# Second pass of a two-layer product by a seven-product block scheme on 768-token chunks

## The chip, the cores and the metric

One core of a Trainium2 chip. The metric is the device time of one execution, in microseconds (us); lower is better. Engines: PE (TensorE, matrix products), DVE (VectorE), ACT (ScalarE), POOL (GpSimd) and SP (SyncE, which here issues every DMA).

## What is computed

```python
scores = scale * np.matmul(q, k.transpose(0, 1, 3, 2))      # 8 batches, 8 heads, 576 tokens, head size 64
scores = np.where(mask, scores + bias[None], -1e9)           # causal window of 128, a linear bias per head
attn = softmax(scores); attn_out = np.matmul(attn, v)
x = attn_out.transpose(0, 2, 1, 3).reshape(4608, 512)
h = x @ w_in                                                 # 512 x 2048
sp = np.maximum(h, 0.0) + np.log1p(np.exp(-np.abs(h)))
out = (h * erf(sp)) @ w_out                                  # 2048 x 512
```

The weights arrive as 64-bit floats. Every operand of the two products is split into a high and a low float32r part, and a product is three: high by high, high by low, low by high.

## The kernel before

Attention is 48 steps, one for each of 12 chunks of 384 tokens and 4 pairs of heads: scores on PE (L614; the first eight steps have other forms), bias and minimum on DVE (L648), exponentials on ACT (L656), the inverse of the sums on DVE (L670, L671), the normalisation on POOL (L679), a transpose on DVE (L696), the product with v on PE (L718). Its output x goes to DRAM and, for the first chunks, stays in SBUF.

The 2048 columns of the first product are 16 ff tiles of 128, too many for SBUF beside attention, so they are done in two passes. **Pass one** runs beside attention and after it: 12 chunks x `NF1` = 7 tiles = 84 units of 384 tokens. A unit has its first products (`unit`, 12 matrix products, L926), a copy from PSUM (L908 on ACT or L912 on DVE), for a round of five units softplus and erf on ACT with their table loads (L963, L965), the product with h, the split into `gh` and `gl` on DVE (L975, L912, L979), and the second products (`products`, 9 for a unit, L997) that add to one PSUM bank for each 128 tokens. The partial outputs go to DRAM (`pd`). **Pass two** does the other 9 tiles on 9 chunks of 512 tokens, 81 units of 12 first and 12 second products of 512 columns, reads the partial outputs back, adds them (L1019) and stores (L1024).

`Weights.prepare` turns a 128 x 512 tile of weights into its two halves: two operations on ACT (L802, or POOL; L809), shift, sign and addition on DVE (L812, L814, L816), the high half (L908, L912 or POOL) and the low half on DVE (L823). Pass one's fourteen tiles come at the start; pass two's eighteen come when attention has closed its pools (`gone`), and stay in SBUF.

The order on every engine is fixed when the program is built. Code makes operations with costs, reads, writes and a due time `at`; `Plan.run` gives each free engine the operation that is ready and due first. Every engine then runs its own list in order and waits by semaphores; SP's list holds all DMA issues. A tile of a pool waits until the one that had its place is read. PSUM has eight banks: `o0` to `o2` for sums, `h` for first products in pass one, four `s` for attention and then for pass two.

Of the kernel before, what the change touches and what calls it, by code (L numbers as in the profile page):

```python
# [19 lines left out]
P = 128  # L20
# [22 lines left out]
PB, XB, OB, TB = 3, 3, 3, 2  # L43
QB, VB = 4, 2
# [12 lines left out]
W2A, W2B = 60, 2.0  # L57
# [94 lines left out]
SUB = ALU.subtract  # L152
# [228 lines left out]
def dve(n, fast=False):  # L381
    return 0.1 + n * (0.00054 if fast else 0.00108)
# [391 lines left out]
class Weights:  # L774
# [10 lines left out]
    def prepare(self, which, f, at, after=()):  # L785
# [4 lines left out]
        r = Buf(self.stage, [P, DM], I32, "wt", 2, f"wu{nm}")  # L790
        t = Buf(self.stage, [P, DM], I32, "wt", 2, f"wt{nm}")
# [5 lines left out]
        flt = lambda x: x.all.bitcast(F32)  # L797
        V = nc.vector

        def lower(e):  # L800
            if e == "Act":
                nc.scalar.mul(flt(q), words(1).bitcast(F32), 2.0**-112)  # L802
            else:
                nc.gpsimd.tensor_scalar(flt(q), words(1).bitcast(F32), 2.0**-112, 1.0, op0=ALU.mult, op1=ALU.mult)
# [3 lines left out]
        def units(e):  # L808
# [8 lines left out]
        pool, tag = self.place(which, f)  # L817
        hi = Buf(pool, [P, DM], F32R, "h" + tag, 1, "wh" + nm)
        lo = Buf(pool, [P, DM], F32R, "l" + tag, 1, "wl" + nm)
        op({**({} if f < POOLH else {"Act": act(DM), "DVE": dve(DM, True)}), "Pool": pool_cast(DM)},  # L820
           lambda e: Moe.copy(self, e, hi.all, flt(t)),
            r=[t, *after], w=[hi], at=at)
        op({"DVE": dve(DM)}, lambda e: V.tensor_tensor(lo.all, flt(t), hi.all, SUB),  # L823
            r=[t, hi, *after], w=[lo], at=at)
        self.t[which, f] = (hi, lo)


class Moe:
# [4 lines left out]
    def __init__(self, tc, plan, ctx, x_dram, part_dram, out):  # L833
# [11 lines left out]
        for nf, size, width, tail in zip((NF1, NF - NF1), UPR, (CH, CH2), ((), TAIL)):  # L845
            n = nf * (self.nt // width) - sum(tail)
            self.rounds += [size] * (n // size) + [n % size] * (n % size > 0) + [*tail]

    def one_pass(self, weights, first, width, accs, time, x_pool=None, after=()):

        self.first, self.width = first, width
        self.x_pool, self.after = x_pool or self.xp, list(after)
# [19 lines left out]
    def load_x(self, c, at):  # L872
        nc, op, W = self.nc, self.plan.op, self.width
        if self.first and c in self.raw:
            raw = self.raw[c]
            parts = [p for cc, p in self.direct_parts if cc == c]
            halves = [[p for p in parts if p.at[1] // 2 == k2] for k2 in range(2)]
        else:
            raw = Buf(self.x_pool, [P, NK, W], F32, "xr", 1, f"xr{c}_{int(self.first)}")
            pieces, pos = [], c * W  # L880
            while pos < (c + 1) * W:
                d, off = divmod(pos, CH)
                n = min(CH - off, (c + 1) * W - pos)
                pieces.append((d, off, pos - c * W, n))
                pos += n

            def load(e):
                for d, off, to, n in pieces:
                    nc.sync.dma_start(raw[:, :, to : to + n], self.x_dram[d][:, :, off : off + n])

            op(emit=load, r=[*self.after, *(x for d, *_ in pieces for x in self.x_parts[d])], w=[raw],
               at=at - XL, **dma(P * NK * W * 4, len(pieces)))
            halves = [[raw], [raw]]
        x = []
        for k2 in range(2):
# [3 lines left out]
            op({"DVE": dve(2 * W, True), "Act": act(2 * W), **({} if self.first and c >= POOLX else {"Pool": pool_cast(2 * W)})},  # L899
# [48 lines left out]
    def flush(self):  # L948

        nc, op, W = self.nc, self.plan.op, self.width  # L950
        units, self.round = self.round, []
        V, A, G = nc.vector, nc.scalar, nc.gpsimd
        total = len(units) * W
        pairs = []
        for i, hs in enumerate(self.hs):
            u = units[i * MW // W]
            s = Buf(self.hp, [P, MW], F32, "m", MB, f"s{u['U']}", keep=KS)
            pairs.append((min(MW, total - i * MW), hs, s, u["at"] + MC, u["U"]))
        first = self.first

        def tables(e):
            for n, hs, s, at, U in pairs:
                A.activation(s[:, :n], hs[:, :n], AF.Softplus)  # L963
            for n, hs, s, at, U in pairs:
                A.activation(s[:, :n], s[:, :n], AF.Erf)  # L965
# [4 lines left out]
           r=[p[1] for p in pairs], w=[p[2] for p in pairs], at=pairs[0][3])  # L970
        g = []
        for n, hs, s, at, U in pairs:
            gh = Buf(self.hp, [P, MW], F32R, "m", MB, f"gh{U}", keep=1)
            gl = Buf(self.hp, [P, MW], F32R, "m", MB, f"gl{U}", keep=0)
            op({"DVE": dve(n)}, lambda e, s=s, hs=hs, n=n: V.tensor_tensor(hs[:, :n], s[:, :n], hs[:, :n], ALU.mult),  # L975
                r=[s, hs], w=[hs], at=at)
            op({"DVE": dve(n, True), "Act": act(n), **({} if first and pairs[0][4] >= POOLG else {"Pool": pool_cast(n)})},
# [4 lines left out]
        for j, u in enumerate(units):  # L982
            self.products(u, j * W, g)
# [176 lines left out]
```

## Time and profile before

| | |
|---|---|
| median of three runs | 984.11 us (981.88 to 984.54) |
| profiled execution | span 983.3 us from the first to the last instruction; the page gives no other time of it |
| PE | 955.2 us busy, 97% |
| DVE, ACT, POOL | 561.1, 608.3, 149.3 us busy |
| DMA | 115.09 MB, mean 117 GB/s |

Busy time is that in which an engine has an instruction under way. A matrix product's record runs on into the next one's, so the price of one is the distance between starts. Attention ends at about 400 us, the last first product of pass one is at 520 us.

### The profile page before, as it was taken

Reading aid. Unit: us, or ns where it says so; the run is one execution under the profiler, and the core shown is the slowest. Engines: PE = TensorE matmul, PEld = TensorE weight load, DVE = VectorE, ACT = ScalarE, POOL = GpSimd, SP = SyncE. Lnnn points to the kernel's source line nnn. Section 1 sums busy time; section 2 is a strip of 40 time slices with the busy share of each in tenths; the row PEclk is TensorE's granted clock in tenths of the full one; section 3 lists DMA queues with packets and bytes.
Section 4 is the critical chain, followed back from the end, with each engine's and each line's share of the span. In section 5 each row is a group of like instructions: output and inputs, shape, how many; then the busy total and the mean of one; then the engine's idle time right before and its main releaser. Section 6 shows DMA issues by size and latency. Waiting matters only on the chain.

```text
span 983.3 us, 25856 instructions
## 1 busy us (share of the span) xinstructions
PE 955.2 (97%) x10936; PEld 801.7 (82%) x10936; DVE 561.1 (57%) x1336; ACT 608.3 (62%) x1245; POOL 149.3 (15%) x297
## 2 busy tenths in 40 slices
PE   8788999999999999999999999999999999999997
PEld 6577877888888888989998888888888888888886
DVE  6877885776667666774389434343434343434342
ACT  7878885678667865786688563636363636363552
POOL 3444333333233323000001000000000000000000
PEclk9988999999999999999999999999999999999999
DMA  6675555547555552551034112121212121212021
GB/s 232 217 220 178 171 188 169 184 144 226 180 165 171 184 192 87 199 168 37 33 116 142 64 43 86 43 86 43 87 43 86 43 86 43 86 43 86 1 65 43
DMA packets 52932, 115.09 MB, mean 117 GB/s; under 512 B 5584, under 2 KB 22736, under 8 KB 52816
## 3 DMA queue, kind: packets, MB, share of 16 engines
q1 hardware_dynamic: 52816, 113.43, 36.1%
q8 instruction: 86, 1.41, 0.6%
q14 instruction: 30, 0.25, 0.1%
HBM read 85.10 MB, written 28.31 MB: 115 GB/s over the span
## 4 chain that ended last, share of the span: by engine, by line
PE 81%; ACT 6%; DVE 4%; POOL 3%; DMA 3%; issue 2%; SPq 0%; ACTq 0%; POOLq 0%; DVEq 0%
PE banks L997 37%; PE banks L926 36%; PE banks L718 5%; POOL p L679 3%; PE banks L614 3%; DMA wri<-w_in 2%; ACT p L656 1%; DVE pa L696 1%; ACT s L963 1%; DMA tables<-bias 1%; ACT s L965 1%; ACT L965 1%; ACT L963 1%; ACT L967 0%; ACT wui L809 0%
## 5 line engine op out<-in xcount | busy, mean ns | idle before, releaser
L926 PE MATMUL banks<-xh,whi 128*128 128x384 f32 (+1 forms) x660 | 245.6, 372 | 8.2 <-ACT hs L908 5.5
L926 PE MATMUL banks<-xh,wli 128*128 128x384 f32 (+1 forms) x660 | 240.9, 365 | 1.3 <-DVE wli L823 1.3
L926 PE MATMUL banks<-xl,whi 128*128 128x384 f32 (+1 forms) x660 | 240.7, 365 | 0.0
L997 PE MATMUL banks<-who,gh 128*128 128x512 f32 x576 | 229.6, 399 | 0.5 <-DVE ot L912 0.5
L997 PE MATMUL banks<-wlo,gh 128*128 128x512 f32 x576 | 225.3, 391 | 0.3 <-issue 0.3
L997 PE MATMUL banks<-who,gl 128*128 128x512 f32 x576 | 225.4, 391 | 0.0
L908 ACT COPY hs<-banks 128x384 f32<-128x384 f32 (+2 forms) x127 | 58.4, 468 | 224.0 <-PE banks L926 223.9
L679 POOL TENSOR_SCALAR p<-p,st 128x160 f32<-128x160 f32 (+2 forms) x282 | 139.0, 514 | 228.1 <-DVE st L671 175.4
L926 PEld LDWEIGHTS banks<-xh,whi 128*128 128x128 f32 x660 | 125.1, 190 | 31.1 <-ACT hs L908 7.7
L912 DVE COPY hs<-banks 128x512 f32<-128x512 f32 (+2 forms) x66 | 37.8, 573 | 190.1 <-PE banks L926 170.2
L926 PEld LDWEIGHTS banks<-xl,whi 128*128 128x128 f32 x660 | 125.4, 190 | 15.5
L926 PEld LDWEIGHTS banks<-xh,wli 128*128 128x128 f32 x660 | 125.1, 190 | 14.1 <-DVE wli L823 1.7
L656 ACT ACTIVATE p<-p,st 128x160 f32<-128x160 f32 (+2 forms) x288 | 120.5, 423 | 25.1 <-DVE st L648 23.5
L997 PEld LDWEIGHTS banks<-who,gh 128*128 128x128 f32 x576 | 108.1, 188 | 27.7 <-issue 6.3
L997 PEld LDWEIGHTS banks<-who,gl 128*128 128x128 f32 x576 | 108.1, 188 | 23.5 <-DVE hs L975 0.5
L997 PEld LDWEIGHTS banks<-wlo,gh 128*128 128x128 f32 x576 | 108.1, 188 | 19.3
L975 DVE TENSOR_TENSOR hs<-s,hs 128x768 f32<-128x768 f32 (+1 forms) x106 | 89.9, 884 | 17.3 <-ACT s L965 17.3
L648 DVE CUSTOM_DVE_ANT_0 p<-banks,tables 128x160 f32<-128x160 f32 (+2 forms) x288 | 75.3, 319 | 31.3 <-PE banks L614 30.8
L979 DVE TENSOR_TENSOR gl<-hs,gh 128x768 fp32r<-128x768 f32 (+1 forms) x106 | 91.0, 888 | 0.7
L963 ACT ACTIVATE s<-hs 128x768 f32<-128x768 f32 (+1 forms) x106 | 76.5, 776 | 0.5
L965 ACT ACTIVATE s<-s 128x768 f32<-128x768 f32 (+1 forms) x106 | 76.4, 776 | 0.5
L718 PEld LDWEIGHTS banks<-pa,v 32*64 32x64 f32 x4576 | 59.5, 132 | 14.5 <-issue 8.6
(66 smaller groups left out, 874.5 us busy)
## 6 DMA issues: line engine op xcount, KB each, us to landing
v<-v_b SPq DMA_DIRECT2D x24, 512.0 KB, 4.0
xr<-xd SPq DMA_DIRECT2D x14, 768.0 KB, 4.9
qk<-qk SPq DMA_DIRECT2D x24, 400.0 KB, 4.1
pd<-ot SPq DMA_DIRECT2D x36, 256.0 KB, 3.8
ot<-pd SPq DMA_DIRECT2D x36, 256.0 KB, 3.4
wri<-w_in SPq DMA_DIRECT2D x16, 512.0 KB, 4.2
qk<-qk SPq DMA_DIRECT2D x16, 512.0 KB, 4.6
wro<-w_out SPq DMA_DIRECT2D x16, 512.0 KB, 4.1
```

Of the source, the lines that this page charges most:

```text
L648: nc.vector.tensor_tensor_reduce(out=dst(j), in0=cut(ps[j].all), in1=cut(table[:, half * j + c0 : half * j + c0 + n]), scale=-0.125, scala ...
L656: nc.scalar.activation(dst(j), dst(j), AF.Exp, bias=low[:, j : j + 1], scale=-1.0, accum_out=total[:, j : j + 1])
L679: (nc.vector if e == "DVE" else nc.gpsimd).tensor_scalar(dst, dst, totals[t][:, j : j + 1], 1.0, op0=ALU.mult, op1=ALU.mult)
L718: nc.tensor.matmul(whole[64 * j : 64 * j + 64, first + a, 32 * t0 : 32 * (t0 + n)], lhsT=y.v[rows, 128 * slot + 64 * j : 128 * slot + 64 * ...
L908: self.nc.scalar.copy(out, src)
L912: self.nc.vector.tensor_copy(out, src)
L926: nc.tensor.matmul(ps[:, :W], lhsT=ww[:, cs], rhs=xx[:, k], start=(k2 + k + n == 0), stop=(k2 + k + n == 4),)
L963: A.activation(s[:, :n], hs[:, :n], AF.Softplus)
L965: A.activation(s[:, :n], s[:, :n], AF.Erf)
L975: op({"DVE": dve(n)}, lambda e, s=s, hs=hs, n=n: V.tensor_tensor(hs[:, :n], s[:, :n], hs[:, :n], ALU.mult), r=[s, hs], w=[hs], at=at)
L979: op({"DVE": dve(n)}, lambda e, gh=gh, gl=gl, hs=hs, n=n: V.tensor_tensor(gl[:, :n], hs[:, :n], gh[:, :n], SUB), r=[hs, gh], w=[gl], at=at)
L997: nc.tensor.matmul(po.all, lhsT=gg[:, cs], rhs=w.all, start=(u["start"] and n == 0), stop=(u["end"] and n == 2),)
```

## The change

`NF1` is 6, so pass one has 72 units. Pass two works on 6 chunks of 768 tokens and 5 pairs of ff tiles, 30 rounds. For a round the first product of a pair (256 columns of w_in) with 768 tokens is cut into blocks in all three dimensions: 128 columns, 256 of the 512 inner rows, 384 tokens. Eight block products become seven, on sums and differences of blocks. The sums of w_in are made once for a pair, beside attention (`Weights.pair`: four sums, then `split`), and written split to DRAM with the split w_out; each round reads 1.84 MB of `wi` and 1.05 MB of `wo` (`fetch`, with three places for each). The differences of x are made once for a chunk (`load_blocks`). The seven products go into two banks `z`; products that share a sum add to a bank whose content has been copied out between them. Six banks hold the sums of the second product. Parts of x and every third `wi` lie where pass one's weights were.

```diff
-NF1 = 7
-UPR = (5, 3)
+NF1 = 6
+UPR = 5
+NP = (NF - NF1) // 2
+LEFT = {"A11": (0, 512), "A12": (256, 768), "S1": (1024, 1536), "S2": (1280, 1792),
+        "S3": (2048, 2560), "S4": (2304, 2816), "A22": (3072, 3328)}
...
+    def split(self, name, src, n, r, to, at):
+        nc, op = self.nc, self.plan.op
+        wb = Buf(self.stage, [P, 2, DM], F32R, "wb", WB, name)
+        op({"Act": act(n), "DVE": dve(n, True), "Pool": pool_cast(n)},
+           lambda e: Moe.copy(self, e, wb[:, 0, :n], src()), r=r, w=[wb], at=at)
+        op({"DVE": dve(n)}, lambda e: nc.vector.tensor_tensor(wb[:, 1, :n], src(), wb[:, 0, :n], SUB),
+           r=[*r, wb], w=[wb], at=at)
+        op(emit=lambda e: nc.sync.dma_start(
+            to.ap.rearrange("p (two n) -> p two n", two=2), wb[:, :, :n].bitcast(F32)),
+           r=[wb], w=[to], at=at, **dma(2 * P * n * 4))
+
+    def pair(self, p, f, wi, wo, at):
+        t1, t2 = (self.decode(0, f + j, at) for j in range(2))
...
+            eng.tensor_tensor(s1, a21, a22, ADD)
+            eng.tensor_tensor(s2, s1, a11, SUB)
+            eng.tensor_tensor(s3, a11, a21, SUB)
+            eng.tensor_tensor(s4, a12, s2, SUB)
+
+        op({"DVE": 4 * dve(SB), "Pool": 4 * pool_tt(SB)}, add, r=[t1, t2], w=[sums], at=at)
...
+    def blocks_pass(self, wi, wo, pool, home, gone, time):
+        tags = ["o0", "o1", "o2", "h", "a0", "a1"]
+        R = 0
+        for C in range(self.nt // (2 * CH)):
+            x = self.load_blocks(C, time(R), pool, home, gone)
+            po = [Buf(self.ps, [P, DM], F32, tag, 1, f"q{C}_{tag}") for tag in tags]
+            for p in range(NP):
+                own, over = home["wi"] if R % 3 == 2 else (Buf(pool, [P, 14 * SB], F32, "wi", 2, f"wi{R}"), [])
+                a = self.fetch(wi[p], own, over * (R == 2), 14 * SB, gone, time(R) - WL)
+                own = Buf(pool, [P, 4 * DM], F32, "wo", 3, f"wo{R}")
+                b = self.fetch(wo[p], own, [], 4 * DM, gone, time(R) - WL + 0.6 * TR)
+                self.pair(C, p, R, x, a, b, po, time(R))
+                R += 1
...
+        z, v, u = (Buf(self.ps, [P, 512], F32, "z", 2, f"{k}{R}") for k in "zvu")
+        product(z, "A11", "B11", True)
+        read(z, h[0][0])
+        product(v, "A12", "B21", True)
+        add(v, h[0][0])
+        product(z, "S2", "T2", False)
+        read(z, h[0][1])
+        product(u, "S1", "T1", True)
+        product(z, "S3", "T3", False)
+        read(z, h[1][1])
+        add(u, h[1][1])
+        product(u, "S4", "B22", False)
+        add(u, h[0][1])
+        product(z, "A22", "T4", False)
+        read(z, h[1][0])
+        g = self.activate([(MW, hs[j], h[j], at + MC, f"{R}_{j}") for j in range(2)])
...
+                    for n, (gg, k) in enumerate(((gh, 0), (gh, 1), (gl, 0))):
+                        nc.tensor.matmul(
+                            po[t].all, lhsT=gg[:, cs], rhs=w[k],
+                            start=(first and j + n == 0), stop=(last and j + n == 3),
...
-        home = self.op_ if self.first or t % 2 else self.x_pool
-        ot = Buf(home, [P, DM], F32, "o", OB, f"ot{T}_{u['U']}")
+        ot = Buf(self.op_, [P, DM], F32, "o", OB, f"ot{T}_{u['U']}")
...
+    for p in range(NP):
+        w1.later = [attention.loaded[min(WN + p * WD, len(attention.loaded) - 1)]]
+        w1.pair(p, NF1 + 2 * p, wi[p], wo[p], W2A + p * W2B)
```

`product` is six matrix products of 384 columns. A round's PE work stands in the order like this. Before, PE in pass two: a unit's first products on the halves of x (`xh`, `xl`), then another unit's second products.

```order
L926 MATMUL banks<-xh_1_10085,whi_7254 128x512
L926 MATMUL banks<-xl_1_10087,whi_7254 128x512
L926 MATMUL banks<-xh_1_10085,wli_7261 128x512
L997 MATMUL banks<-who_8248,gh_10046 128x512
L997 MATMUL banks<-wlo_8259,gh_10046 128x512
L997 MATMUL banks<-who_8248,gl_10056 128x512
```

Now, PE in a round of pass two (L1158 are block products, `yh`, `yl` and `w_551` the parts of x, `wi` the weights; L1196 second products in groups of three):

```order
L1158 MATMUL banks<-yl_2_10286,wi_10301 128x384
L1158 MATMUL banks<-yh_2_10243,wi_10301 128x384
L1158 MATMUL banks<-w_551,wi_10301 128x384 x6
L1196 MATMUL banks<-wo_10333,gh_0_10479 128x512 x2
L1196 MATMUL banks<-wo_10333,gl_0_10486 128x512
L1158 MATMUL banks<-w_551,wi_10301 128x384 x6
L1196 MATMUL banks<-wo_10333,gh_0_10479 128x512 x2
L1196 MATMUL banks<-wo_10333,gl_0_10486 128x512
L1196 MATMUL banks<-wo_10333,gh_1_10484 128x512 x2
L1196 MATMUL banks<-wo_10333,gl_1_10494 128x512
L1158 MATMUL banks<-w_551,wi_10301 128x384 x12
```

The second products of a round stand among the first products of the round two later, one or two groups between block products, the other eight behind them.

DVE in an attention step, before, from the inverse of one step to the transpose of the next (the rows of L648 between them are left out where they repeat):

```order
L696 STREAM_TRANSPOSE pa_5744<-p_5591 128x960
L648 ISA p_5730,st_5731<-banks,tables_320_857 128x160
L648 ISA st_5731 128x1
```
```order
L670 TENSOR_SCALAR st_5731<-st_5731 128x6
L671 RECIPROCAL st_5731<-st_5731 128x6
L518 COPY xs_5845<-banks 128x384
L696 STREAM_TRANSPOSE pa_5877<-p_5730 128x960
```

Now, DVE at such a place (L859 makes low halves of pass two's weights, L1032 and L1036 are the old L975 and L979, L717 the transpose):

```order
L717 STREAM_TRANSPOSE pa_4624<-p_4442 128x960
L691 TENSOR_SCALAR st_4580<-st_4580 128x6
L692 RECIPROCAL st_4580<-st_4580 128x6
L1036 TENSOR_TENSOR gl_4643<-hs_1_4092,gh_4567 128x768
L1032 TENSOR_TENSOR hs_2_4354<-s_4360,hs_2_4354 128x384
L859 TENSOR_TENSOR wb_4427<-ws_4385,wb_4427 128x512
L859 TENSOR_TENSOR wc_4588<-ws_4385,wc_4588 128x512
L717 STREAM_TRANSPOSE pa_4723<-p_4579 128x960
```

Between an inverse and the transpose behind it, while POOL normalises, there now stand operations of the units and of pass two's weights.

SP at the end, before (`ot` with `pd` is the load of a partial output, `out_dram` a store):

```order
L1018 DMA ot_164_10979<-pd_114 128x512
L1018 DMA ot_164_10984<-pd_115 128x512
L1024 DMA out_dram<-ot_164_10654 32x512 x2
L1024 DMA out_dram<-ot_164_10654 64x512
L1024 DMA out_dram<-ot_164_10659 128x512
L1024 DMA out_dram<-ot_164_10979 64x512 x2
L1024 DMA out_dram<-ot_164_10984 128x512
```

And now:

```order
L1079 DMA out_dram<-ot_29_11255 32x512
L1079 DMA out_dram<-ot_29_11263 64x512
L1079 DMA out_dram<-ot_29_11263 32x512 x2
L1079 DMA out_dram<-ot_29_11271 32x512 x2
L1079 DMA out_dram<-ot_29_11271 64x512
L1073 DMA ot_29_11576<-pd_113 128x512
L1073 DMA ot_29_11578<-pd_114 128x512
L1073 DMA ot_29_11580<-pd_115 128x512
L1079 DMA out_dram<-ot_29_11576 128x512
L1079 DMA out_dram<-ot_29_11578 64x512 x2
L1079 DMA out_dram<-ot_29_11580 128x512
```

The last three loads of partial outputs stood ahead of the last stores; now they stand behind the stores of the first half of the chunk, whose buffers they take.

## Rows read from the trace of the kernel before

**Rows 1.** Busy time by stage: stretch, length, busy us (instructions) of each engine, granted clock, DMA.
```profile
core 0: us, PE busy (x) PEld busy (x) DVE busy (x) ACT busy (x) POOL busy (x), PEclk, DMA share, GB/s
0.00:100.00 100.00, 82.62 (x1602) 68.63 (x1603) 75.82 (x276) 76.22 (x232) 41.00 (x80) 0.90 0.66 213
...
405.00:517.00 112.00, 111.65 (x559) 100.70 (x558) 69.86 (x106) 82.70 (x122) 2.31 (x2) 1.00 0.32 111
517.00:958.00 441.00, 441.00 (x1949) 365.58 (x1949) 202.35 (x269) 227.75 (x286) 3.29 (x3) 1.00 0.21 66
```
**Rows 2.** Waits of PE from 400 us: who for whom, us, times, longest.
```profile
PE banks L926 <- ACT hs L908: 0.3, 1, 0.3
```
**Rows 3.** Timeline of PE, the first products of two units in pass one.
```profile
403.03 0.34 PE L926 MATMUL banks<-xh,whi 128*128 128x384 f32 x1
...
407.22 0.33 PE L926 MATMUL banks<-xh,whi 128*128 128x384 f32 x1
```
**Rows 4.** Chain that ended last, its end: start us, us, what.
```profile
956.21 2.72 PE banks L926 x12
958.93 19.05 PE banks L997 x84
...
978.00 0.69 DVE ot L1019
```
**Rows 5.** Timeline of PE, scores of the 17th and the last attention step.
```profile
129.18 1.05 PE L614 MATMUL banks<-qk 64*32 64x160 f32 x48
...
388.15 1.05 PE L614 MATMUL banks<-qk 64*32 64x160 f32 x48
```
**Rows 6.** Busy time by stretch in the attention stage.
```profile
88.00:100.00 12.00, 12.00 (x210) 10.61 (x209) 9.85 (x28) 8.41 (x24) 6.69 (x11) 1.00 0.69 217
100.00:120.00 20.00, 19.25 (x394) 15.75 (x392) 16.83 (x47) 18.76 (x45) 5.99 (x10) 1.00 0.45 143
120.00:130.00 10.00, 7.86 (x204) 6.26 (x188) 9.01 (x24) 8.00 (x21) 4.50 (x6) 1.00 0.70 239
130.00:150.00 20.00, 19.89 (x329) 16.49 (x313) 16.64 (x47) 14.90 (x37) 7.43 (x13) 1.00 0.58 181
...
129.18:388.15 258.97, 256.81 (x5876) 214.45 (x5875) 173.16 (x586) 177.08 (x512) 90.68 (x192) 1.00 0.55 172
```
**Rows 7.** Waits of DVE from 129 to 388 us.
```profile
DVE p L648 <- PE banks L614: 27.7, 15, 4.5
DVE pa L696 <- POOL p L679: 20.7, 21, 1.6
```
**Rows 8.** Groups of instructions by line and shape: copies from PSUM.
```profile
L908 ACT COPY hs<-banks 128x384 f32<-128x384 f32 x60 | 28.4, 474 | 37.3 <-PE banks L926 37.3
L912 DVE COPY hs<-banks 128x384 f32<-128x384 f32 x24 | 13.3, 554 | 29.5 <-PE banks L926 29.3
```
**Rows 9.** Timeline of SP near the end: issues of eleven stores.
```profile
944.04 5.79 SPq L1024 DMA_DIRECT2D out_dram<-ot  x11
```
**Rows 10.** DMA issues: how many, KB each, median us to landing.
```profile
ot<-pd SPq DMA_DIRECT2D x36, 256.0 KB, 3.4
...
out_dram<-ot SPq DMA_DIRECT2D x14, 256.0 KB, 2.1
```
**Rows 11.** Groups of DVE: decoding of weights and low halves.
```profile
L823 DVE TENSOR_TENSOR wlo<-wto,who 128x512 fp32r<-128x512 f32 x16 | 11.3, 709 | 0.3
L814 DVE SCALAR_TENSOR_TENSOR wti<-wqi,wti 128x512 int32<-128x512 int32 x16 | 11.2, 701 | 0.4
L816 DVE CUSTOM_DVE_ANT_0 wti<-wti,wui 128x1024 uint16<-128x1024 uint16 x16 | 11.2, 698 | 4.1 <-ACT wui L809 3.4
L812 DVE TENSOR_SCALAR wti<-wqi 128x512 int32<-128x512 int32 x16 | 7.0, 437 | 0.6
L979 DVE TENSOR_TENSOR gl<-hs,gh 128x256 fp32r<-128x256 f32 x3 | 1.3, 421 | 0.0
```
**Rows 12.** Groups of POOL, from 100 to 150 us and from 200 to 388 us.
```profile
L679 POOL TENSOR_SCALAR p<-p,st 128x160 f32<-128x160 f32 x25 | 15.8, 650 | 22.6 <-DVE st L671 14.5 <-ACT wuo L809 8.1
...
L679 POOL TENSOR_SCALAR p<-p,st 128x160 f32<-128x160 f32 x141 | 65.1, 483 | 123.2 <-DVE st L671 97.1 <-ACT gh L908 17.4 <-ACT ot L908 8.8
```

More of the change, by code (lines that the diff above doesn't have):

```diff
@@ L783, in __init__, with decode @@
         self.t = {}
-    def prepare(self, which, f, at, after=()):
+    def decode(self, which, f, at):
         nc, op = self.nc, self.plan.op
@@ L844, in __init__, with one_pass @@
         self.rounds = []
[L845 to L852, printed above, removed]
+        n = NF1 * (self.nt // CH)
+        self.rounds += [UPR] * (n // UPR) + [n % UPR] * (n % UPR > 0)
+    def one_pass(self, weights, accs, time):
+        self.first, width = True, CH
+        self.width, self.after = width, []
         fs = weights.ffs
@@ L873, in load_x @@
         nc, op, W = self.nc, self.plan.op, self.width
-        if self.first and c in self.raw:
+        if c in self.raw:
             raw = self.raw[c]
@@ L878, in load_x @@
         else:
[L879 to L892, printed above, removed]
+            raw = Buf(self.xp, [P, NK, W], F32, "xr", 1, f"xr{c}")
+            op(emit=lambda e: nc.sync.dma_start(raw.all, self.x_dram[c].ap), r=self.x_parts[c], w=[raw],
+               at=at - XL, **dma(P * NK * W * 4))
             halves = [[raw], [raw]]
@@ L898, in load_x @@
             src = slice(2 * k2, 2 * k2 + 2)
-            op({"DVE": dve(2 * W, True), "Act": act(2 * W), **({} if self.first and c >= POOLX else {"Pool": pool_cast(2 * W)})},
+            op({"DVE": dve(2 * W, True), "Act": act(2 * W), **({} if c >= POOLX else {"Pool": pool_cast(2 * W)})},
                lambda e, hi=hi, src=src: self.copy(e, hi.all, raw[:, src]), r=halves[k2], w=[hi], at=at - XS)
@@ L948, in flush, with activate @@
     def flush(self):
-        nc, op, W = self.nc, self.plan.op, self.width
+        W = self.width
         units, self.round = self.round, []
-        V, A, G = nc.vector, nc.scalar, nc.gpsimd
         total = len(units) * W
[L954 to L958, printed above, removed]
+        g = self.activate([
+            (min(MW, total - i * MW), hs, [hs], units[i * MW // W]["at"] + MC, f"{units[i * MW // W]['U']}")
+            for i, hs in enumerate(self.hs)])
+        for j, u in enumerate(units):
+            self.products(u, j * W, g)
+    def activate(self, tiles):
+        nc, op = self.nc, self.plan.op
+        V, A = nc.vector, nc.scalar
         first = self.first
+        pairs = [(n, hs, Buf(self.hp, [P, MW], F32, "m", MB, f"s{nm}", keep=KS), at, nm) for n, hs, _, at, nm in tiles]
+        read = [r for _, _, r, _, _ in tiles]
         def tables(e):
-            for n, hs, s, at, U in pairs:
+            for n, hs, s, at, nm in pairs:
                 A.activation(s[:, :n], hs[:, :n], AF.Softplus)
-            for n, hs, s, at, U in pairs:
+            for n, hs, s, at, nm in pairs:
                 A.activation(s[:, :n], s[:, :n], AF.Erf)
@@ L981, in flush @@
             g.append((gh, gl))
-        for j, u in enumerate(units):
-            self.products(u, j * W, g)
+        return g
     def products(self, u, pos, g):
@@ L1017, in store @@
         else:
-            op(emit=lambda e: nc.sync.dma_start(ot.all, part.ap), r=[part, *self.after], w=[ot], at=at - 10, **dma(nbytes))
+            op(emit=lambda e: nc.sync.dma_start(ot.all, part.ap), r=[part], w=[ot], at=at - 10, **dma(nbytes))
             op({"DVE": dve(DM)}, lambda e: nc.vector.tensor_tensor(
@@ L1053, in tile_kernel, with place @@
     t1 = t0 + n1 * TM
-    w1 = Weights(nc, plan, lambda k, f: (w1p, f"{k}_{f}"), stage, w_in, w_out, range(NF1), attention.loaded[3:4])
+    whole = Buf(w1p, [P, 4 * NF1 * DM], F32R, "w1", 1, "w1")
+    slots = {}
+    def place(k, f):
+        s0 = (2 * k * NF1 + 2 * f) * DM
+        for j in range(2):
+            slots[s0 // DM + j] = Part(whole, slice(None), slice(s0 + j * DM, s0 + (j + 1) * DM))
+        return slots[s0 // DM], slots[s0 // DM + 1]
+    w1 = Weights(nc, plan, place, stage, w_in, w_out, range(NF1), attention.loaded[3:4])
     for k in range(2):
```

181 lines of the change are left out of this document (144 added, 37 removed).

## The prediction

> **What bounds the kernel now.** I read first the busy time by stage [rows 1]: while attention runs beside pass one and after it, TensorE (PE) is the full engine. From 405 to 517 us it is busy 111.65 of 112 us and from 517 to 958 us all 441; DVE and ACT have a quarter to a half of that time free. Before 100 us it is not: 82.6 of 100, at a granted clock of 0.90. Then the waits of PE from 400 us on [rows 2]: one, of 0.3 us. So behind the attention the time is the number of matrix products by what one takes. The timeline gives that price: in pass one a unit (12 products of 384 columns, 9 of 512) starts 4.19 us after the one before [rows 3]. In pass two, twelve products of 512 columns take 2.72 us, 0.2267 each [rows 4], and so a 384-column product in the mixture takes (4.19 - 9 x 0.2267)/12 = 0.179. The chain's end [rows 4] shows the tail: the last product is over at 978.0, the span at 983.3.
>
> The attention stage is the other half. It has 48 steps; the scores of the 17th start at 129.18 and those of the last at 388.15 [rows 5], so 31 steps take 259 us. In that stretch, the last line of [rows 6], PE is busy 256.8 us, DVE 173.2, ACT 177.1. DVE waits in it, among other things, 27.7 us for scores and 20.7 us in front of its transposes for POOL's normalisation [rows 7].
>
> **The change, part by part.** The sum is made against the profiled span, 983.3 us, which is 0.8 under the median of the runs, 984.11.
>
> *Products.* Pass one does 72 units, not 84: -12 x 4.19 = -50.3 us. Pass two did 9 chunks x 9 tiles = 81 units of 24 products of 512 columns: 81 x 24 x 0.2267 = 440.7. It will do 6 chunks x 5 pairs = 30 rounds, each 7 block products x 6 matrix products of 384 columns and 2 x 6 x 3 of 512: 42 x 0.179 + 36 x 0.2267 = 15.68, in all 470.4: +29.7. Net -20.6. If a 384-column product cost in proportion to its columns (0.170) a round would be 15.30 and the net -32; that is the lower bound. I take -20.6, since the mixture of widths in pass one is the nearest row.
>
> *Reads between block products.* The seven products share two banks, so a product that adds to a bank waits until its last content is copied out. The order puts one or two groups of three second products (0.68 each) or another block product (6 x 0.179 = 1.07) between a product and the next on its bank: 1.4 to 2.1 us. A copy of 384 columns takes 0.474 us on ACT, 0.554 on DVE [rows 8], and copy and addition together 1.03. The second products that fill lie two rounds back, so their activation chain has a round of 15.7 us in hand. 0, bounds 0 and +15 (0.5 a round). The work of DVE on the additions is beside PE: it is half idle there [rows 1].
>
> *Start of pass two and ends of chunks.* In the first two rounds no second products are left, and four block products stand in a row: each waits for a copy of its bank, some 1 us in all (0 to +5). At the end of a chunk the sums of tokens 3 to 5 need partial outputs whose loads wait on three buffers, behind a 1 MB weight load: the accumulator is wanted about when they come. +1 for five chunks (0 to +10).
>
> *Tail.* This one is in the order. The stores of the last chunk's first three tiles are eight transfers, and the loads for the other three tiles stand behind them on SP and reuse their buffers. With E the end of the last product, the first sum is done at E - 2.6; eleven such issues took 5.79 us [rows 9], eight take 4.2, so SP reaches the first load at E + 1.6; the third load waits for the last of those stores to land (about E + 3.5), takes 3.4 [rows 10], then comes an addition of 0.69 [rows 4] and a store of 2.1 [rows 10] with its issue: E + 10. Before it was 5.3 behind E. +5 (bounds +2 and +8).
>
> *First 129 us.* At the 17th step's scores the order has 11.5 first and 3 second units behind it, not 14.5 and 5.3: 11 us of the 50.3 lie here, where PE is not full [rows 1]. They come back only as far as the steps get shorter. DVE and ACT, each 76 of 100 us busy here, lose a seventh of pass one's weights and the activations of those units. I take +3, bounds 0 and +11.
>
> *Attention stage.* Here the work on pass two's weights lands, which today is done from 400 us on. Nineteen more tiles are decoded in the 31 steps at 0.437 + 0.701 + 0.698 = 1.84 us of DVE [rows 11]; 25 lower halves of 512 at 0.709, five of 256 and twenty sums at 0.42 (the row of 256 columns), and sixteen copies at about 0.437, the price of the shift: 35 + 18 + 10 + 7 = 70, some 65 as starts overlap. DVE then has 238 of 259 us, 92%. ACT gets about 27 more, 79%. Units per step hardly change (40 of each kind, before 39.5 and 39.7), so PE's work stays. What does PE do beside so full a DVE? The nearest rows are 88 to 150 us [rows 6]: DVE at 82% with PE full, at 83% with PE at 99.4%, at 90% with PE at 79%, the last with one wait of 1.9 us behind a block of table work on ACT. Over those 62 us PE idles 4.8%, in the long stretch 0.8%; the difference on 259 us is 10 us. I take half, +5, because the new work is spread evenly and the 90% piece holds that one wait; bounds 0 and +23.
>
> POOL's normalisation, which stands between DVE's two halves of a step, takes 650 ns an operation at 100 to 150 us and 483 from 200 us on [rows 12]. [...]
>
> Sum: 983.3 - 20.6 + 0 + 1 + 1 + 5 + 3 + 5 = 977.7; with the 0.8 to the median, **978.5 us**. DMA costs nothing here: the new writes and reads are prefetched by two rounds; if that cover goes, it is the second rival.
>
> **Rivals.** (1) *DVE becomes the bound of the attention stage* (slower). Place: the transposes behind the normalisation. Its point: DVE's work and the transposes' wait must fit in 259 us, so it decides from 238 us of work on, and the estimate stands right there. Price: at 650 instead of 483 ns, six operations a step cost 1.0 us more, 31 in all; if half of that lengthens the wait, 240 + 20.7 + 15.5 = 276, +17 instead of +5: 990. For it: the 90% piece. Against: PE full at 82 to 88%, and that the waits for scores can be filled.
> (2) *DMA becomes the bound of pass two* (slower). 30 rounds read 1.84 + 1.05 MB, with x, partial sums and output 115 MB; at 239 GB/s, the highest rate shown [rows 6], that is 480 us against 470: +10, 988. Against: the engines were then busy 0.70 of the time, which leaves a third. Copies of banks that come late every round have the same sign (up to +15) and are counted here.
> (3) *Nothing stalls* and 384 columns cost between the two prices: 983.3 - 26 + 5 + 3 = 965 or so. For it: pass two of today runs without a gap.
>
> **How the numbers follow.** What a measurement can tell from no change is about 0.3%, 3 us: 981.2 to 987.1. The forecast has 0.46; its own range is 971 to 986, so 0.36 faster and 0.10 same. Rival 1 has 0.30 (0.28 slower, 0.02 same), rival 2 0.09 (0.07 slower, 0.02 same), rival 3 0.15, faster. Faster 0.51, same 0.14, slower 0.35. The range is 963 to 1000: it leaves out the extreme bounds of the products below and of the attention with the banks above.
>
> **What would show it.** Right: rounds of pass two 15.7 us apart, PE without idle time from the end of attention; scores of steps 17 and 48 still about 259 us apart, PE over 97% busy between them; about 10 us from the last product to the end. Wrong: those steps 270 us or more apart with DVE's waits on POOL grown (rival 1); a DMA share over 0.9 and PE waiting on weights in pass two (rival 2); many PE waits on copies of banks. If the first 17 steps take as long as now, the +3 was too small.

## The result, and the profile after

The changed kernel takes 990.77 us (median of 20 executions, 984.83 to 998.99) against 984.59 us for the kernel before (20 executions, 979.87 to 988.64). The ratio is 1.0066, 95% interval 1.0046 to 1.0086: **slower by 0.7%**, where 978.5 was forecast. The profiled execution is the fastest of the twenty: 984.83 us, span 983.0. The one of before lies near its median: span 983.3, and with the 1.8 us that other executions take around their span some 985.1 (an estimate). So the two traces differ by -0.3 us where the medians differ by +6.2. Piece by piece:

| piece | before | changed | difference | forecast |
|---|---|---|---|---|
| start to 17th scores | 129.2 | 117.75 | -11.4 | -8 |
| 17th to 48th scores | 259.0 | 274.5 | +15.5 | +5 |
| 48th scores to the last product's end | 589.85 | 580.7 | -9.2 | -7.6 |
| last product's end to the end | 5.3 | 10.1 | +4.8 | +5 |
| span | 983.3 | 983.0 | -0.3 | -5.6 |

(Forecast of the first and third row: the net -20.6 of the products, 11 of it in the first row, +3 there, +1 and +1 in the third.)

Busy time by stretch of the changed kernel; the columns are those of [rows 1], and the first line answers to the last of [rows 6]:

```profile
117.75:392.24 274.49, 262.49 (x5886) 216.68 (x5885) 236.65 (x711) 208.46 (x573) 114.50 (x198) 1.00 0.76 253
392.24:500.00 107.76, 107.76 (x787) 96.59 (x787) 52.81 (x84) 62.24 (x96) 6.33 (x13) 1.00 0.43 156
...
483.40:973.00 489.60, 487.16 (x2414) 436.21 (x2412) 260.45 (x359) 286.40 (x365) 0.00 (x0) 1.00 0.59 214
```

In the 31 attention steps PE executes nearly what it did (5886 products recorded, 5876 before; six of 384 and three of 512 columns more, about 1.7 us), but is idle 12.0 us instead of 2.2 and busy 5.7 us longer. DVE has 237 us of work, as forecast (238), and the DMA share went from 0.55 to 0.76. From there on PE is full. What PE waits for in the 31 steps (for whom, us in total, times, longest):

```profile
PE banks L635 <- issue: 4.8, 5, 1.2
PE banks L739 <- DVE st L669: 2.7, 5, 1.0
PE banks L977 <- issue: 1.9, 3, 0.9
PE banks L1053 <- issue: 1.4, 1, 1.4
PE banks L739 <- issue: 0.7, 1, 0.7
```

8.8 us of it is "issue": PE stands still and no semaphore ends it. Before, the same stretch had 1.3 us:

```profile
PE banks L718 <- issue: 1.3, 3, 0.7
```

On the timeline of PE these gaps lie inside groups of products that have already begun (the last bracket is the idle time ahead of a row):

```profile
140.87 0.48 PE L635 MATMUL banks<-qk 64*32 64x160 f32 x8 [1.25 <-issue]
177.32 0.47 PE L635 MATMUL banks<-qk 64*32 64x160 f32 x7 [1.13 <-issue]
184.17 0.34 PE L739 MATMUL banks<-pa,v 32*64 32x32 f32 x13 [0.72 <-issue]
201.32 0.34 PE L977 MATMUL banks<-xl,w 128*128 128x384 f32 x1 [0.54 <-issue]
```

Forty of the 48 score products have run at 140 us, then nothing for 1.25 us, then the other eight. The stretches from one such gap to the next:

```profile
140.87:177.32 36.45, 35.00 (x764) 28.73 (x764) 31.46 (x94) 29.53 (x76) 15.94 (x31) 1.00 0.80 262
177.32:184.17 6.85, 6.13 (x127) 5.12 (x128) 6.56 (x19) 4.60 (x12) 0.50 (x1) 1.00 0.83 318
184.17:201.32 17.15, 16.59 (x382) 13.37 (x382) 13.05 (x45) 11.56 (x39) 7.21 (x13) 1.00 0.64 192
201.32:214.80 13.48, 12.61 (x255) 10.31 (x254) 10.03 (x26) 9.75 (x23) 6.31 (x13) 1.00 0.95 312
```

764, 127, 382 and 255 products, each with its weight load, are 6, 1, 3 and 2 times 127.4. The page's list of DMA queues says what comes in such portions:

```profile
q1 hardware_dynamic: 58640, 214.36, 62.8%
q8 instruction: 87, 1.43, 0.6%
```

87 packets of 16.4 KB; PE's 11080 products and 11080 weight loads, divided by 87, are 254.7 instructions a packet, or 127.4 pairs. So the gaps would stand where a new packet of PE's instructions begins. The trace dates the packets of q8 and bears this out: all ten "issue" gaps of the 31 steps end 2.2 to 2.4 us after one of them starts (the first starts at 138.53, PE goes on at 140.87), and from gap to gap as many packets start as the multiples above. The packets that end gaps are not slower than others (0.9 to 1.0 us each); they start late. Counted from the product with which the packet before began, packets start after 0.7 us in the median where the DMA share over the next 2 us is under 0.3 (7 packets), and after 2.4 us where it is over 0.9 (14 packets). The DMA engines around the first gap (rows of 1 us each):

```profile
138.00:139.00 1.00, 1.00 (x28) 0.75 (x34) 0.97 (x4) 0.96 (x3) 0.23 (x1) 1.00 1.03 395
139.00:140.00 1.00, 0.62 (x32) 0.29 (x16) 1.00 (x3) 0.98 (x3) 1.00 (x2) 1.00 1.17 369
140.00:141.00 1.00, 0.13 (x4) 0.14 (x8) 0.96 (x4) 0.99 (x2) 1.00 (x2) 1.00 0.92 223
```

The DMA share is 0.92 to 1.17 in the rows in which PE stands still for 1.25 us.

How much of the +15.5 is this? The added "issue" gaps alone are 7.6 us. A product's record can run on into such a gap (the last product ahead of the first one starts at 139.32 and is recorded until 139.62, where the starts before it lie 7 ns apart), so starts tell more: against the median distance of the same two kinds of products, delays of over 0.1 us that end 2.1 to 2.6 us behind the start of a packet add up to 13.1 us, before to 3.2: some 10 us (an estimate). Added waits for DVE (2.7 against 0.5 us) and the 1.7 us of added products are most of the rest.

For 36 of the 46 packets of the 31 steps no "issue" gap shows, for ten one does.

### The profile page after: what moved, and what is told of

Its sections match the earlier page's. It is cut to its first block, busy times and chain, and to the rows that moved or that the text cites. A ratio compares the mean times of both kernels' runs of the same rounds, so it can differ in the third digit from the quotient of the medians.

```text
span 983.0 us, 26558 instructions
## 1 busy us (share of the span) xinstructions
PE 938.8 (95%) x11080; PEld 815.2 (83%) x11080; DVE 629.5 (64%) x1468; ACT 638.5 (65%) x1290; POOL 169.6 (17%) x304
## 4 chain that ended last, share of the span: by engine, by line
PE 63%; DMA 2%; DVE 1%; POOL 1%; issue 0%; SPq 0%; ACT 0%; DVEq 0%; POOLq 0%
PE banks L1196 24%; PE banks L1158 21%; PE banks L1053 8%; PE banks L977 7%; PE banks L739 2%; DMA ot<-pd 2%; PE banks L635 1%; DMA out_dram<-ot 1%; POOL p L700 1%; DVE ot L1074 0%; DVE p L669 0%; SPq L1079 0%; DVE pa L717 0%; DVE hs L963 0%; SPq L1102 0%
## 5 line engine op out<-in xcount | busy, mean ns | idle before, releaser
L1196 PE MATMUL banks<-wo,gh 128*128 128x512 f32 x720 | 223.6, 391 | 1.3 <-DVE ot L1074 1.3
L977 PE MATMUL banks<-xh,w 128*128 128x384 f32 x576 | 170.3, 351 | 8.8 <-ACT hs L959 6.1
L1196 PEld LDWEIGHTS banks<-wo,gh 128*128 128x128 f32 x720 | 133.1, 188 | 22.6 <-DVE ot L1074 2.4
L1053 PE MATMUL banks<-w,gh 128*128 128x512 f32 x432 | 139.9, 405 | 3.1 <-DVE gh L963 1.7
L1196 PE MATMUL banks<-wo,gl 128*128 128x512 f32 x360 | 141.6, 393 | 0.0
L977 PEld LDWEIGHTS banks<-xh,w 128*128 128x128 f32 x576 | 108.2, 192 | 19.3 <-ACT hs L959 7.6
L1032 DVE TENSOR_TENSOR hs<-s,hs 128x768 f32<-128x768 f32 (+1 forms) x103 | 89.5, 899 | 30.0 <-ACT s L1022 30.0
L977 PE MATMUL banks<-xl,w 128*128 128x384 f32 x288 | 98.5, 342 | 0.5 <-issue 0.5
L1158 PE MATMUL banks<-w,wi 128*128 128x384 f32 x480 | 94.7, 336 | 0.7 <-DVE hs L963 0.7
L1036 DVE TENSOR_TENSOR gl<-hs,gh 128x768 fp32r<-128x768 f32 (+1 forms) x103 | 91.3, 910 | 5.4 <-ACT gh L959 4.2
L1158 PEld LDWEIGHTS banks<-w,wi 128*128 128x128 f32 x480 | 85.1, 188 | 5.7 <-DVE hs L963 1.0
L1053 PE MATMUL banks<-w,gl 128*128 128x512 f32 x216 | 86.0, 398 | 0.1
L1196 PEld LDWEIGHTS banks<-wo,gl 128*128 128x128 f32 x360 | 67.5, 187 | 14.3
```

The lines of the kernel that those rows point to most:

```text
L977: nc.tensor.matmul(ps[:, :W], lhsT=ww[:, cs], rhs=xx[:, k], start=(k2 + k + n == 0), stop=(k2 + k + n == 4),)
L1036: op({"DVE": dve(n)}, lambda e, gh=gh, gl=gl, hs=hs, n=n: V.tensor_tensor(gl[:, :n], hs[:, :n], gh[:, :n], SUB), r=[hs, gh], w=[gl], at=at)
L1053: nc.tensor.matmul(po.all, lhsT=gg[:, cs], rhs=w.all, start=(u["start"] and n == 0), stop=(u["end"] and n == 2),)
L1158: nc.tensor.matmul(ps[:, :CH], lhsT=w(o), rhs=y[:, k], start=(begin and k + n == 0), stop=(k + n == 3), skip_group_check=not begin)
L1196: nc.tensor.matmul(po[t].all, lhsT=gg[:, cs], rhs=w[k], start=(first and j + n == 0), stop=(last and j + n == 3),)
```

## The experiments

Theory A: DVE's added work makes the steps longer. Theory B: DVE's two-input instructions do, by slowing POOL's normalisation (in the 31 steps an operation of it took 492 ns before, 591 in the changed kernel). Theory C: the added transfers are late themselves. Theory D, formed after the first four runs: PE runs out of instructions because of the transfers. In e3, e4, e5 and b1 PE's instructions and their order are those of the kernel that they start from. Each ratio is to executions of the kernel before made alongside; the last three columns are of one profiled execution each.

| run | us | ratio to before (95%) | 31 steps | GB/s in them | "issue" gaps of PE in them |
|---|---|---|---|---|---|
| before | 984.6 | 1 | 259.0 | 172 | 1.3 |
| changed | 990.8 | 1.0066 (1.0046 to 1.0086) | 274.5 | 253 | 8.8 |
| e1_again | 990.3 | 1.0054 (1.0037 to 1.0071) | 275.3 | 252 | 9.5 |
| e3_dve_light | 988.7 | 1.0048 (1.0029 to 1.0067) | 277.3 | 250 | 12.3 |
| e4_no_stores | 986.7 | 1.0023 (1.0001 to 1.0046) | 274.0 | 211 | 6.6 |
| e5_one_input | 990.4 | 1.0060 (1.0038 to 1.0081) | 276.9 | 250 | 7.6 |
| b1_traffic | 997.2 | 1.0123 (1.0095 to 1.0151) | 273.8 | 266 | 6.8 |
| g0_all_after | 995.5 | 1.0106 (1.0083 to 1.0130) | 260.5 | 175 | 2.9 |
| g2_three_after | 1005.8 | 1.0206 (1.0180 to 1.0232) | 283.0 | 196 | 9.3 |
| e6_tail | 987.3 | 1.0023 (1.0001 to 1.0046) | 278.3 | 249 | 10.7 |
| h2_two_before | 985.2 | 0.9994 (0.9974 to 1.0015) | 272.4 | 203 | 9.6 |
| h1_one_before | 980.0 | 0.9958 (0.9941 to 0.9975) | 265.8 | 190 | 5.9 |

**e1_again**: no edit.

> The changed kernel once more, for a profile of an execution nearer to its median (990.8 us; the execution profiled first was the fastest of twenty, 984.8). All theories: 985 to 999 us. Theory A (DVE's added work makes the attention steps longer): the 31 steps from the 17th to the 48th scores take 270 us or more again, and what this execution has above 984.8 lies before the end of the attention, with a granted clock under 1.00 there; the rounds of pass two and the tail (10 us) are as in the first profile. Theory C (DMA bounds pass two or the loads): the excess lies in pass two or beside waits on transfers.

Its profile (span 983.4) is once more of an execution faster than the median, so it does not show where the others spend their 6 us. It shows that the 31 steps repeat, and the gaps with them: 1.7 us ahead of the last eight score products at 141, 1.17 ahead of the last seven at 177. In the 20 timed executions of the changed kernel time goes with the granted clock (0.978 to 0.987, correlation -0.75, 1.1 us for each 0.001).

**e3_dve_light**: in the decoding and splitting of pass two's weights,

```
- V.scalar_tensor_tensor(t, q, -(1 << 31), t, bitwise_and, bitwise_or)
- V.tensor_tensor(t, t, r, ALU.add)
- nc.vector.tensor_tensor(wb[:, 1, :n], src(), wb[:, 0, :n], SUB)
- dma_start(to, wb[:, :, :n])
+ for k in range(2): dma_start(to.ap[:, k * n : k * n + n], wb[:, 0, :n])
```

> The changed kernel, but the weights of pass two are decoded without the OR and the addition, and their lower halves are not computed (the upper half is stored twice): 48 us of DVE's work gone from the stretch of the 31 steps, all with two inputs, every other instruction and every transfer's bytes as before. Theory A (DVE's load) and theory B (POOL's normalisation and DVE's two-input instructions exclude each other): the 31 steps go from 274.5 back to 259 to 264 us, DVE's busy share there from 86% to under 75%, time 972 to 979 us. Theory C (the added transfers): 274 us for the steps, time within 3 us of the changed kernel.

Its 31 steps, busy time by stretch:

```profile
119.42:396.68 277.26, 264.96 (x5886) 218.83 (x5885) 192.72 (x641) 207.38 (x573) 97.54 (x198) 0.98 0.77 250
```

And what PE waits for in them:

```profile
PE banks L635 <- issue: 6.0, 5, 2.8
PE banks L980 <- issue: 3.4, 2, 1.9
PE banks L739 <- issue: 1.7, 2, 1.0
PE banks L1056 <- issue: 1.2, 1, 1.2
```

44 us of DVE's work are gone, DVE is busy 70%, PE no longer waits for DVE in them, and the steps take 277 us. (The granted clock, 0.98 in their mean, can have cost them some 5 us; without that they would still take 272, an estimate.) Theory A falls, and with it the first rival of the prediction. (The time fell by about 2 us, too little to tell from the changed kernel.) This trace also shows what a gap costs behind itself, here around the 2.75 us ahead of the products at 181.24:

```profile
179.00:181.20 2.20, 0.00 (x0) 0.00 (x0) 0.36 (x1) 2.18 (x4) 0.36 (x1) 1.00 1.01 391
181.20:182.20 1.00, 0.96 (x8) 0.48 (x9) 0.19 (x1) 0.78 (x1) 0.00 (x0) 0.55 0.73 279
182.20:184.00 1.80, 1.80 (x6) 1.51 (x6) 1.77 (x13) 1.56 (x7) 0.00 (x0) 0.50 0.64 156
184.00:185.50 1.50, 1.50 (x8) 1.50 (x8) 1.47 (x3) 0.19 (x2) 0.00 (x0) 0.76 0.85 300
185.50:188.00 2.50, 2.50 (x47) 1.96 (x46) 2.45 (x4) 0.00 (x0) 0.00 (x0) 1.00 0.39 137
```

The granted clock is 1.00 while PE stands still, goes to 0.50 as PE begins again, and is at 1.00 throughout only in the row from 185.5 on: by the clock of the three rows between, PE loses 0.45 + 0.90 + 0.36 = 1.7 us more (an estimate). The length of a gap alone does not decide: in this trace one of 1.04 us was followed by such a fall, and in e1_again one of 2.01 us was not (its 31 steps have a mean granted clock of 1.00). So gaps may spread the executions; that they are what does is not shown.

**e4_no_stores** (`first`: the store is of the first pair, the fetch from its tensors):

```
- op(emit=lambda e: nc.sync.dma_start(to, wb[:, :, :n]), ...)
+ op(emit=lambda e: first and nc.sync.dma_start(to, wb[:, :, :n]), ...)
- nc.sync.dma_start(w.all, src[0].whole.ap)
+ nc.sync.dma_start(w.all, first[0].whole.ap)
```

> The changed kernel, but only the first pair's split weights are stored and pass two reads that pair in every round: 11.6 MB fewer written in the attention stage, DVE's, ACT's and POOL's work and pass two's reads unchanged. Theories A and B: the 31 steps still take 270 us or more, time within 3 us of the changed kernel. Theory C: the steps fall to under 265 us and the time by 8 us or more.

Between the two: 4 us less than the changed kernel, the steps as long as in the changed kernel. At 211 GB/s the gaps are fewer (6.6 us) but the longest is there, 3.12 us ahead of the same last seven score products. PE waited for no transfer of data (its other waits are 3.6 us for DVE): theory C as put falls, and what the transfers do must go by another way. That was theory D.

**e5_one_input**:

```
- V.scalar_tensor_tensor(t, q, -(1 << 31), t, ...); V.tensor_tensor(t, t, r, ALU.add)
+ V.transpose(t, q); V.transpose(t, r)
- nc.vector.tensor_tensor(wb[:, 1, :n], src(), wb[:, 0, :n], SUB)
+ nc.vector.transpose(wb[:, 1, :n], src())
```

> The changed kernel, but in the decoding of pass two's weights the OR and the addition, and the subtractions that give the lower halves, are each replaced by a 32x32-block transpose of the same 512 columns: one input instead of two, about the same DVE time (960 columns take 1177 ns, so 512 about 0.65 us against 0.70). Theory B (lock between POOL and two-input DVE instructions): POOL's normalisation falls from 591 to about 500 ns in the 31 steps, DVE's wait for it from 23 to under 15 us, the steps to under 265 us, time 977 to 981. Theory A (DVE's load): the steps stay at 270 us or more and the time within 4 us of the changed kernel, whatever the normalisation takes.

POOL's normalisation in the 31 steps, of the changed kernel:

```profile
L700 POOL TENSOR_SCALAR p<-p,st 128x160 f32<-128x160 f32 x186 | 106.7, 591 | 157.1 <-DVE st L692 122.9 <-ACT hs L959 19.9 <-ACT wb L959 6.1
```

and of e5_one_input:

```profile
L700 POOL TENSOR_SCALAR p<-p,st 128x160 f32<-128x160 f32 x186 | 90.6, 507 | 174.9 <-DVE st L692 151.5 <-ACT hs L960 12.7 <-ACT wb L960 6.1
```

DVE's wait for it, in the changed kernel and in e5_one_input:

```profile
DVE pa L717 <- POOL p L700: 23.2, 25, 1.7
DVE pa L717 <- POOL p L700: 13.4, 16, 1.7
```

With one input instead of two the normalisation falls from 591 to 507 ns, and DVE's wait for it from 23.2 to 13.4 us. By what way the two engines' instructions hinder each other is not shown. The shorter normalisation was worth nothing: 276.9 us and 990.4 (the clock in the steps is 0.98 here too, so 272 us without its falls, an estimate). Theory B falls as a cause of the time.

**b1_traffic**: the kernel before, with two transfers a step that nobody needs.

```
+ def echo(self, tile, parts, size):
+     if self.n >= PLAIN:
+         to = dram.tile([P, size])
+         op({"SP": 0.0}, lambda e: nc.sync.dma_start(to, tile[:, :size]), r=parts, ...)
```

> The kernel BEFORE, with transfers alone added: in each of the 40 later attention steps the q/k tile and the v tile, once loaded, are also written to a DRAM buffer that nobody reads (some 0.9 MB a step, 29 MB in the 31 steps; the change adds 25 MB there). No computation is added and PE, DVE, ACT and POOL run the same instructions in the same order. Theory D (new: PE runs out of instructions, because its instruction packets wait behind data on DMA engines that are full): in the 31 steps gaps of 0.4 to 3 us appear on PE that no semaphore ends, inside groups of small products, some 8 us in all, against 1.3 us before; the steps go from 259 to 268 us or more, and the time rises by 6 us or more. Theories A and B (DVE's load, DVE's lock with POOL): steps 259 to 262, time within 2 us of the kernel before.

Its 31 steps, and the stretches between its first three gaps, busy time by stretch:

```profile
126.75:400.54 273.79, 262.03 (x5877) 216.17 (x5876) 171.91 (x585) 176.86 (x511) 87.77 (x190) 0.99 0.80 266
...
158.73:165.03 6.30, 5.56 (x128) 4.66 (x129) 2.99 (x15) 3.10 (x13) 1.55 (x5) 1.00 0.84 290
165.03:236.96 71.93, 67.32 (x1530) 55.60 (x1530) 46.27 (x153) 50.93 (x139) 23.77 (x50) 1.00 0.82 274
```

What PE waits for in the 31 steps:

```profile
PE banks L621 <- issue: 4.3, 4, 1.7
PE banks L725 <- issue: 2.5, 2, 1.8
PE banks L621 <- ACT xs L521: 1.5, 1, 1.5
PE banks L933 <- ACT hs L915: 1.2, 1, 1.2
```

The second and the third of these gaps on PE's timeline:

```profile
165.03 0.32 PE L725 MATMUL banks<-pa,v 32*64 32x64 f32 x10 [0.74 <-issue]
236.96 1.02 PE L621 MATMUL banks<-qk 64*32 64x160 f32 x40 [1.74 <-issue]
```

Traffic alone, without a single added computation, makes the 31 steps 14.8 us longer, with PE's busy time up by 5.2 us and gaps 128 and 1530 (12 times 127.5) products apart: the same signature, and all six "issue" gaps end 2.2 to 2.5 us after a packet starts. The gaps themselves are 5.5 us more than before. PE also waits 4.5 us for ACT and DVE, 0.5 before: part of the 14.8 us comes from the traffic by another way, not followed here (an echo also keeps its tile until it is read). The kernel before has its longest such gap at the same instruction, on PE's timeline:

```profile
165.76 0.32 PE L718 MATMUL banks<-pa,v 32*64 32x64 f32 x10 [0.73 <-issue]
```

Theory D holds for the gaps.

**g0_all_after** and **g2_three_after**: the raw loads of a pair wait for the output of a chosen attention step; in g2 the steps are (16, 28, 47, 47, 47).

```
- w1.later = [attention.loaded[min(WN + p * WD, len(attention.loaded) - 1)]]
+ w1.later = [attention.done[(47, 47, 47, 47, 47)[p]]]
```

> The changed kernel; all five pairs of pass two's weights are loaded, decoded, split and stored after the last attention step instead of during it (gate of their raw loads: the store of the last attention output). Theory D: the 31 steps return to 258 to 264 us with under 3 us of PE gaps without a cause; after attention PE runs products of 384 and 512 columns, few instructions a microsecond, so full DMA engines cost it little there; the time is 972 to 980 us unless pass two must wait for its weights (DVE and ACT have about 55 and 45 us free between attention and pass two, against 70 and 27 us of work, and each later pair is needed 16 us after the one before), which would give up to 10 us back. If neither DVE's load nor the transfers matter, the steps stay at 274 us.

> As the one before, but two of the five pairs are prepared during the attention (from its steps 17 and 29 on) and three after it. Theory D: between the changed kernel and the other: the 31 steps take 262 to 269 us, time 976 to 984; no wait of pass two for weights.

With the preparation behind it, the attention is back at 260.5 us, as theory D has it. Busy time by stretch of g0_all_after:

```profile
118.37:378.83 260.46, 257.27 (x5877) 214.37 (x5876) 174.63 (x586) 183.59 (x525) 87.81 (x186) 1.00 0.58 175
378.83:500.00 121.17, 113.38 (x787) 97.70 (x788) 97.06 (x170) 87.64 (x143) 10.50 (x17) 0.97 0.78 281
```

The second line is the control: DMA share 0.78, more than in the changed kernel's attention, and PE stands still for no "issue" in it. PE starts 787 products there in 121 us, 6.5 a microsecond instead of 21, so a packet lasts 20 us. But the forecast for the time was wrong: PE then waits for DVE (4.7 us at once, for a lower half of an activation) and runs at a clock of 0.97, and from the last scores to the last product it takes 603 us instead of 581. g2 missed altogether: its attention takes 283.0 us, partly since the order puts more of pass one into it (269.5 us of PE), with gaps of 9.3 us at only 196 GB/s, and behind it PE waits 5.2 us for one lower half. In both the planner's `at` puts the preparation ahead of pass one's later activations on DVE.

**e6_tail** (in the last chunk only; `sums` lies in a slot of the wi tiles that is free by then):

```
- ot = Buf(self.op_, [P, DM], F32, "o", OB, ...)
+ ot = Part(self.sums, slice(None), slice(DM * t, DM * t + DM))
```

> The changed kernel; the last chunk's six partial outputs are loaded into one buffer of their own (the slot of a weight tile that is free by then) instead of three shared buffers, so no load waits for a store. My reading of the tail: from E + 10.1 to E + 5.3 to 6, time 4 to 5 us less than the changed kernel, 986. Rival: the stores at the end are bound by SP's issues alone, so nothing is gained, 990 to 991.

From the last product's end (977.2) to the end it takes 6.5 us instead of 10.1; the median is 3.5 under the changed kernel's (4 to 5 were expected). The chain of the changed kernel shows the store and the load that are gone:

```profile
973.67 2.23 DMA out_dram<-ot
...
975.95 2.87 DMA ot<-pd
...
979.03 0.69 DVE ot L1074
```

**h1_one_before** and **h2_two_before**: e6_tail with gates at (20, 47, 47, 47, 47) and (16, 28, 47, 47, 47), and

```
- W2A, W2B = 150, 30.0
+ W2A, W2B = 330, 15.5
```

> The changed kernel with the tail of e6_tail, one pair of pass two's weights prepared during the attention and four behind it, and the preparation given lower priority than pass one's activations (in g0_all_after and g2_three_after it went ahead of them on DVE, and PE waited for copies and lower halves: 4.7 and 5.2 us at one place, 0.5 to 2 at many). Theory D: the 31 steps take 259 to 265 us, with under 4 us of causeless PE gaps; from the end of attention to the last product about 580 to 585 us; tail 6.5 us; time 970 to 979 us, under both kernels. If the preparation behind the attention holds PE up whatever its priority, it is 585 to 595 again and the time 982 to 990.

> As the one before with two pairs during the attention and three behind it. Theory D: 31 steps 261 to 268 us, 580 us from the end of attention to the last product, time 972 to 982 us; more causeless PE gaps than with one pair.

h1_one_before beats both kernels: 980.0, 0.4% under the kernel before, 1.1% under the changed one; of these 10.8 us, 3.5 are e6_tail's. Its busy time by stretch:

```profile
119.33:385.12 265.79, 258.77 (x5880) 215.12 (x5879) 189.75 (x616) 185.67 (x531) 93.54 (x188) 1.00 0.61 190
385.12:500.00 114.88, 111.94 (x800) 98.43 (x800) 86.75 (x153) 78.12 (x126) 8.54 (x15) 1.00 0.75 259
```

The 31 steps take 265.8 us (1 over what was expected), with 5.9 us of gaps (under 4 expected); behind them it is 588 us to the last product, 3 more than expected and in the range of the stated rival; the time is 1 us over its range. h2_two_before missed by 3 us: 272.4 us of steps, 9.6 us of gaps.

## Why the prediction was wrong

The forecast was 12.3 us too low: 5.3 of it in the span (977.7 against 983.0), 7.0 in the step from the span to the median. The 5.3 are the 10.5 that the attention stage had too little, less 5 that the first and the third row of the table came out better.

- **Products, reads between block products, start of pass two, ends of chunks**: right. From the third on, rounds start 15.6 to 15.7 us apart (15.68 forecast) but for three of 15.8 to 16.8. PE's only waits after the attention came at the start of pass two, for copies (1.0 us, +1 forecast), and at the ends of two chunks, for additions (1.3, +1 forecast):

```profile
PE banks L1196 <- DVE ot L1074: 1.3, 2, 0.9
PE banks L1158 <- DVE hs L963: 0.7, 1, 0.7
PE banks L1158 <- ACT hs L959: 0.3, 1, 0.3
```

Twelve 384-column products in a row take 2.10 us in the chain that ended last, 0.175 each, not 0.179.
- **First 129 us**: the +3 did not come: -11.4 against -8. That the first and the third row add up to just the net of the products, -20.6, is chance.
- **Tail**: right: 10.1 us against E + 10.
- **Attention stage, the term of +5: this is the step that failed.** It measured +15.5. The prediction priced it by how full DVE would be, with the pieces from 88 to 150 us as nearest rows [rows 6]. DVE's work came out as computed (237 us), but e3 shows that it was not what mattered: PE stood still for instruction packets that started late (after 2.4 us in the median where the DMA share was over 0.9, after 0.7 where it was under 0.3). The nearest rows could not price either: none of PE's waits in them ended at DVE (2.1 us ended at ACT's copies, 0.5 at another of ACT, 0.3 was "issue"), and their DMA share does not go with PE's idle time (0.69 with PE full, 0.45 and 0.70 with idle time). The sign was in the 31 steps of before, in three "issue" gaps of 1.3 us in all, each ending 2.2 to 2.5 us after a packet of q8 starts; no term was made of them.
- **"DMA costs nothing here"**: wrong. Transfers were costed as data: are they landed when wanted? PE waited for none. That they also delay PE's instructions was in no term. Some 25 MB (253 GB/s over 274.5 us against 172 over 259) were added where PE starts 21 products a microsecond (7 from 392 to 500 us, 5 from 483 us on), and b1 shows 14.8 us for about as much traffic (28 MB).
- **The 0.8 us to the median, taken over from the kernel before**: wrong by 7, the other step that failed. The median lies 7.8 us above the profiled span: 1.8 around that span and 5.9 because the execution profiled is the fastest. No profile of an execution of the changed kernel near its median was had, but e6_tail, the same kernel up to its last chunk, comes close: its 985.5 us and the 3.6 of its shorter tail make 989 (an estimate). Against the first profile its 17th scores come 2.3 us later (at 120.1) and its 31 steps take 3.8 us more, at a granted clock of 0.99 where the first had 1.00. So in that execution the excess lies in the attention and ahead of it; that gaps and the clock behind them make it in the others is argued, not shown.
- **The rivals**: the first named nearly the right length for the steps (+17) and 990, by a mechanism that e3 and e5 refute: its number is luck. Its price of 650 ns an operation of the normalisation was an estimate: 591 were measured, and DVE's wait for it went from 20.7 to 23.2 us. The second had the right resource in the wrong place: pass two, with a DMA share of 0.59, waits for no weights.

Open: mean traffic does not by itself rank the gaps (9.6 us at 203 GB/s in h2_two_before, 6.8 at 266 in b1_traffic), so the moments at which transfers meet the packets may matter; that was not tried apart. Nor is it shown what makes PE's busy time longer beyond the added products (4 us in the changed kernel; 5.2 in b1_traffic, where none were added); the records of products that run on before a gap are a part of it.

## What to carry to other kernels

A transfer that nobody waits for can still cost time: 14.8 us of the 31 steps in b1_traffic, where PE starts 21 products a microsecond beside a DMA share of 0.80. Before moving transfers into such a stretch, read its DMA share beside the engine's instructions a microsecond, and look for waits marked "issue" inside groups of products. Background work is worth trying where instructions are few and long, at a priority under the work that feeds the bound engine: in g0_all_after from 379 to 500 us (6.5 products a microsecond, DMA share 0.78) it left PE without "issue" gaps, but PE waited 4.7 us for one lower half; at a lower priority, with one pair still in the attention and with the shorter tail, h1_one_before took 980.0 us. Where a term rests on "the nearest rows", read first what ended the idle time in them: here it was not the engine whose load was priced.

## What the runs showed of the hardware

In the changed kernel the queue of instructions carried 87 packets of 16.4 KB, one for 127.4 of PE's products with their weight loads. After a packet's start it took 2.2 to 2.4 us until PE went on, at all ten "issue" gaps of the changed kernel's steps. Packets started later in that kernel, by the median 2.4 instead of 0.7 us, where the DMA share was over 0.9 instead of under 0.3. At a share of 1.03 (182 to 183 us) PE stood still, in a gap of 3.12 us (e4_no_stores); in one stretch with a share of 0.78 and 6.5 products a microsecond, no "issue" gap showed (g0_all_after, 379 to 500 us). After a gap of 2.75 us the granted clock was 0.50 to 0.76 in the rows of the next 4.3 us (e3_dve_light). A 32x32-block transpose in place of a two-input DVE instruction shortened POOL's neighbouring instruction from 591 to 507 ns (changed kernel against e5_one_input).
